# The branch for tokens past an expert's 512th, moved from behind the last expert to ahead of it, with a prefetch hint for TensorE

## The chip, the cores and the metric

One core of one Trainium2 chip runs the kernel. The metric is the device time of one execution in microseconds (us). The engines are TensorE (PE; PEld is its weight load), VectorE (DVE), ScalarE (ACT), GpSimd (POOL) and SyncE (SP, which here only issues DMAs). Each engine has a sequencer that takes its instructions in order: branches, register loads and semaphore waits are done by the sequencer itself, and the profile shows them under the engine's name with a q (PEldq, DVEq, ACTq, POOLq, SPq).

## The reference

```python
def reference(**kwargs):
    ...
    attn_out = _attn_ref(**attn_kwargs)          # windowed causal attention, window 64, 4 x 8 heads x 576 x 64
    x = np.ascontiguousarray(attn_out.transpose(0, 2, 1, 3)).reshape(B * S, H * D)   # 2304 x 512
    x = _moe_ref(x=x, **moe_kwargs)              # relu(x @ w_in) ** 2 @ w_out, d_ff 2048
    return _moe2_ref(x=x, **moe2_kwargs)
def _moe2_ref(x, w_gate, w1, w2):                # 8 experts, each 512 -> 1024 -> 512
    ...
    for e in range(E):
        mask = expert_idx == e                   # expert_idx = argmax of x @ w_gate
        if not mask.any():
            continue
        xe = x[mask]
        h = np.maximum(xe @ w1[e], 0.0)
        ye = h @ w2[e]
        out[mask] = gate_w[mask, None] * ye
    return out.astype(np.float32)
```

## The kernel before

The first two thirds of the program compute the attention and the dense layer and store its result in HBM, and fill a table `tab` that lists the tokens of each expert. What follows, from about 560 us on, is the mixture of experts, and the change lies there.

Every product runs as three matmuls (`mm3`, L167 to L169), because each fp32 number is kept as a rounded part and a rest: rounded by rounded, rounded by rest, rest by rounded. The weights of the next expert are loaded by SP, rounded by ACT (L276), and their rests are made by DVE or POOL (L277), into units of four buffers that two experts in turn use (`wsp[e]`).

`group(e, ...)` computes one expert for up to 512 tokens. It makes eight passes f: `up(f)` (12 matmuls into a PSUM tile h, with the tokens along the free axis), `relu(f)` (ACT writes the rounded part `ggh`, L770, then DVE the rest `ggl`, L771) and `down(f - 1)` (for each of four token tiles t = 3, 2, 1, 0 three matmuls into the PSUM tiles y). TensorE runs `up(f)` ahead of `down(f - 1)`, so ACT and DVE have the time of one `down` or `up` for their part. How wide `up` runs (256, 352, 448 or 512 tokens) and whether a tile of `down` is needed is decided at run time by the expert's token count n, with `tc.If` (L754, L789): the register with n has been loaded on TensorE alone, ahead of the first expert (L1006). Where a tile isn't needed, one tiny matmul with `nil` stands for it.

After `group`, `scatter` is called for the four tiles: DVE multiplies y by the gate weight into an SBUF tile s (L808), and POOL writes its rows to `out` with an indirect DMA (L809).

Experts can have more than 512 tokens. The count of the fullest expert that the groups have to do is in `most`. Behind the last expert stands a condition that every engine evaluates for itself (L1056): it loads `most` into a register and, where it is over 512, runs `more(e, n)` for each expert concerned; that code loads the weights again and works off the rest in tiles of 128 in a loop. With these inputs no count is over 512, so every engine jumps over that code. In the branch that is taken instead, each engine only waits for its own earlier work and raises the semaphores by what the skipped code would have added. POOL does so for the software DMA queues too, and waits for their transfers first; then comes the end of the program (L1097): SP waits for all semaphores, and all engines meet at a barrier behind a DRAIN.

The order of this stage is the order in which the code is written (`tc.manual_schedule()`); the semaphore waits are put in by the framework, which counts what the conditional code may have touched.

Of the kernel before, what the change touches and what calls it, by code (L numbers as in the profile page):

```python
# [19 lines left out]
P = 128  # L20
# [29 lines left out]
def kernel(  # L50
# [13 lines left out]
    nc = tc.nc  # L64
    B, _, NB, W, HP = qT.shape
    D = P // 2
    NT, DM = out.shape
    DFF = w_in.shape[1] // 2
    E, _, F1 = w1.shape
# [6 lines left out]
    KMAX = NT // P  # L76
    GROUP = 4 * P
# [65 lines left out]
    tab = cpool.tile([P, E * KMAX, 2], I32, tag="tab", name="tab")  # L143
    cnt = cpool.tile([1, E], I32, tag="cnt", name="cnt")
    most = cpool.tile([1, 1], I32, tag="most", name="most")
# [4 lines left out]
    def psum(tag, bufs):  # L150
        return pr.tile([P, 512], F32, tag, bufs)

    ybanks = [pspool.tile([P, 512], F32, tag=f"y{i}", name=f"y{i}") for i in range(2 * TT)]
# [7 lines left out]
    def halves(h, l, src):  # L161

        nc.scalar.copy(h, src)
        nc.vector.tensor_tensor(l, src, h.bitcast(F32), op=ALU.subtract)  # L164

    def mm3(o, ah, al, bh, bl, first, last):
        nc.tensor.matmul(o, lhsT=ah, rhs=bh, start=first, stop=False)  # L167
        nc.tensor.matmul(o, lhsT=ah, rhs=bl, start=False, stop=False)  # L168
        nc.tensor.matmul(o, lhsT=al, rhs=bh, start=False, stop=last)  # L169
# [74 lines left out]
    wsp, stg, busiest, done = {}, {}, [], {}  # L244
# [435 lines left out]
    def transposed(x, ps=None):  # L680
        if ps is None:
            ps = psum("a", 2)
        for c in range(4):
            nc.tensor.transpose(ps[:, c * P:(c + 1) * P], x[:, c * P:(c + 1) * P], ident)
        return ps


    def tile_of(e, c0, y, new_r, new_g, between):
        h1, l1, h2, l2 = wsp[e]
        xh, xl = (x[:, :, c0:c0 + P] for x in xhl)  # L690
        hps = [psum("h", 2) for _ in range(2)]

        def up(f, ks):
            for kk in ks:
                b_ = slice(kk * F1 + f * 512, kk * F1 + f * 512 + 512)
                mm3(hps[f], xh[:, kk, :], xl[:, kk, :], h1[:, b_], l1[:, b_], kk == 0, kk == KD - 1)

        def relu(f):
            r = new_r()
            done["relu", f] = nc.scalar.activation(r, hps[f], ACTF.Relu)  # L700
            return r

        def turned(r):
            ps = transposed(r)
            h, l = new_g()
            halves(h, l, ps)
            return h, l

        def down(f, ht, cs):
            for c in cs:  # L710
                a = slice(c * P, c * P + P)
                fc = f * 4 + c
                b_ = slice(fc * DM, fc * DM + DM)
                mm3(y, ht[0][:, a], ht[1][:, a], h2[:, b_], l2[:, b_], fc == 0, fc == 7)

        up(0, range(4))
        r0 = relu(0)
        between(1)
        up(1, range(2))
        t0 = turned(r0)  # L720
        between(3)
        up(1, range(2, 4))
        r1 = relu(1)
        between(4)
        down(0, t0, range(2))
        t1 = turned(r1)
        between(5)
        down(0, t0, range(2, 4))
        down(1, t1, range(4))
# [3 lines left out]
    def group(e, c0, new_g, between, n=None, first=None, after=None):  # L733

        h1, l1, h2, l2 = wsp[e]
        ys = ybanks[2:] if n is None else ybanks
        width = GROUP if n is not None else 2 * P
        hid = {}

        def up(f):  # L740
            hid[f] = psum("h", 2)

            def part(m, ks=range(KD)):
                for kk in ks:
                    b_ = slice(kk * F1 + f * P, kk * F1 + f * P + P)
                    xh, xl = (x[:, kk, c0:c0 + m] for x in xhl)
                    mm3(hid[f][:, :m], h1[:, b_], l1[:, b_], xh, xl, kk == 0, kk == KD - 1)

            def least(sizes):
                if len(sizes) == 1:  # L750
                    part(sizes[0])
                    return
                mid = len(sizes) // 2
                with tc.If(n > sizes[mid - 1]) as c:  # L754
                    least(sizes[mid:])
                with c.Else():
                    least(sizes[:mid])

            if n is not None:
                least(WIDTHS)  # L760
            elif f == 0:
                part(width, range(KD // 2))
                first()
                part(width, range(KD // 2, KD))
            else:
                part(width)

        def relu(f):
            h, l = new_g()
            nc.scalar.activation(h[:, :width], hid[f][:, :width], ACTF.Relu)  # L770
            nc.vector.scalar_tensor_tensor(  # L771
                out=l[:, :width], in0=hid[f][:, :width], scalar=0.0, in1=h[:, :width].bitcast(F32),
                op0=ALU.max, op1=ALU.subtract,
            )
            hid[f] = h, l

        def down(f):
            gh, gl = hid[f]
            b_ = slice(f * DM, f * DM + DM)

            def tile_(t):
                a = slice(t * P, t * P + P)
                mm3(ys[t], gh[:, a], gl[:, a], h2[:, b_], l2[:, b_], f == 0, f == 7)

            for t in reversed(range(width // P)):
                if n is None or t == 0:
                    tile_(t)
                    continue
                with tc.If(n > t * P) as c:  # L789
                    tile_(t)  # L790
                with c.Else():

                    nc.tensor.matmul(ys[t][:, :2], lhsT=nil, rhs=nil[:, :2], start=True, stop=True, skip_group_check=True)

        for f in range(8):
            up(f)
            relu(f)
            if f == 7:
                between(f)
            if f:  # L800
                down(f - 1)
            if f < 7:
                between(f)
        down(7)

    def scatter(y, ent, ys):
        if y is not None:
            nc.vector.tensor_scalar_mul(ys, y, ent[:, 1:2].bitcast(F32))  # L808
        i = nc.gpsimd.indirect_dma_start(  # L809
            out=out[:, :], out_offset=bass.IndirectOffsetOnAxis(ap=ent[:, 0:1], axis=0), in_=ys[:], in_offset=None,  # L810
            bounds_check=NT - 1, oob_is_err=False,
        )
        tc.declare_no_dep(i.ins, group="out", reason="no token is in two tiles")
        tc.add_to_no_dep_group("out", i.ins)
# [77 lines left out]
    for g in range(2 * QB, NS * QB):  # L892
        st, j = divmod(g, QB)
# [7 lines left out]
    last = slot[NS - 1, 0]  # L901
# [11 lines left out]
    for i in range(-PRE, len(order) + LA):  # L913
# [6 lines left out]
        if i >= LA:  # L920
            st, f = order[i - LA]
# [25 lines left out]
    def base(e):  # L947

        return 2 * P * (1 - e % 2)

    def tokens_in(x, c):

        ps = transposed(x).rearrange("p (k t) -> p k t", k=KD)
        halves(*(xx[:, :, c:c + P] for xx in xhl), ps)
# [7 lines left out]
    def new_r():  # L962
        return er.tile([P, HP, P], F32, "s", 3).rearrange("p h s -> p (h s)")

    ns = []
# [57 lines left out]
    def next_of(e):  # L1023
        def between(f):
            if e + 1 == E:
                return
            if f == 5:
                expert_in(e + 1, (0, 1) if base(e + 1) == 0 else (2, 3))
            if f == 7:
                expert_in(e + 1, (2, 3) if base(e + 1) == 0 else (0, 1))  # L1030
            split(e + 1, f, TILES)

        return between

    def more(e, n):

        wsp.pop(e)
        for i in range(8):
            wload(e, i)
            wsplit(e, i, TILES)  # L1040
        with tc.For_i(GROUP // P, (n + (P - 1)) // P, 1) as i:
            ent = rpool.tile([P, 2], I32, tag="ent", name=f"ent{e}")
            nc.vector.tensor_copy(ent, tab[:, ds(e * KMAX + i, 1), :])
            x = new_r()
            nc.vector.memset(x, 0.0)
            gather(x, ent[:, 0:1])
            tokens_in(x, 0)
            tile_of(e, 0, ybanks[0], new_r, new_g, lambda j: None)
            scatter(ybanks[0], ent, new_r())

    with tc.manual_schedule():
        for e in range(E):
            group(e, base(e), new_g, next_of(e), n=ns[e])
            for t in reversed(range(GROUP // P)):
                scatter(ybanks[t], tab[:, e * KMAX + t, :], new_r())
        with tc.If(nc.values_load(most[0:1, 0:1], min_val=0, max_val=NT) > GROUP, preferred_fallthrough_block=False):  # L1056
            for e in range(E):
                n = nc.values_load(cnt[0:1, e:e + 1], min_val=0, max_val=NT)
                with tc.If(n > GROUP):
                    more(e, n)  # L1060


# [38 lines left out]
```

## Time and profile before

| | |
|---|---|
| time, median of 3 runs | 857.18 us (856.23 to 858.75) |
| time of the profiled execution | 855.37 us |
| its span, first to last instruction | 853.7 us |
| TensorE busy | 795.4 us (93% of the span) |
| DVE, ACT, POOL busy | 564.3, 388.0, 274.9 us |
| last matmul of the program | starts at 834.86 us |
| last scatter issued by POOL | starts at 838.06 us |

Times within the profile count from the start of the span. The span lies 1.7 us below the time of the same execution, and the profiled execution itself 1.8 us below the median of the three others. A busy share says how long an engine worked, not whether anything waited for it; what bounds a stretch is read from who waits for whom there.

### The profile page before, as it was taken

What the parts mean: (1) busy time and instruction counts of PE and PEld (TensorE: products, weight loads), DVE (VectorE), ACT (ScalarE), POOL (GpSimd) and SP (SyncE); (2) the same over time, 40 slices, a digit from 0 to 9 for tenths busy, and PEclk for the clock granted to TensorE, in tenths of its full rate; (3) what the DMA queues carried; (4) which work ended last, traced back from release to release, by engine and by line L of the source; (5) the groups of instructions that cost most, each with busy time, mean ns of one, the idle gap of its engine ahead of it and who ended that gap; (6) DMA issues with size and microseconds to landing.
All of it is one profiled execution on the core that took longest, in us unless ns stands there. A gap on an engine that the chain in (4) does not pass through costs nothing. (4 is left out here: it accounts for less than half of the span.)

```text
span 853.7 us, 15131 instructions
## 1 busy us (share of the span) xinstructions
PE 795.4 (93%) x5295; PEld 692.1 (81%) x5295; DVE 564.3 (66%) x1293; ACT 388.0 (45%) x1025; POOL 274.9 (32%) x272
## 2 busy tenths in 40 slices
PE   6878889999999999999999999979998999999991
PEld 5767667988889889898888887868887788888880
DVE  6999995794764947649477396558699763534211
ACT  6986644333443443534444344446566543334110
POOL 4425431112131221312211025366666643431201
PEclk9999999999999999999999999989999999999996
DMA  9854643110211111112111046456476644320101
GB/s 266 279 167 132 190 160 101 43 45 26 68 45 55 45 39 63 50 45 57 35 53 38 13 142 194 137 184 209 144 248 195 218 149 148 120 90 2 46 2 45
DMA packets 50859, 91.49 MB, mean 107 GB/s; under 512 B 8220, under 2 KB 24604, under 8 KB 50752
## 3 DMA queue, kind: packets, MB, share of 16 engines
q1 hardware_dynamic: 44688, 80.43, 30.0%
q0 software_dynamic: 6064, 9.63, 3.4%
q8 instruction: 68, 1.11, 0.5%
q14 instruction: 39, 0.32, 0.1%
HBM read 84.59 MB, written 13.81 MB: 115 GB/s over the span
## 5 line engine op out<-in xcount | busy, mean ns | idle before, releaser
L167 PE MATMUL h<-xh,w 128*128 128x256 f32 (+3 forms) x864 | 262.3, 304 | 16.0 <-DVE gl L479 15.5
L168 PE MATMUL h<-xl,w 128*128 128x256 f32 (+3 forms) x864 | 254.7, 295 | 0.3 <-DVE xl L164 0.3
L169 PE MATMUL h<-xh,w 128*128 128x256 f32 (+3 forms) x864 | 254.8, 295 | 0.0
L167 PEld LDWEIGHTS h<-xh,w 128*128 128x128 f32 x864 | 163.9, 190 | 33.6 <-DVE gl L479 19.7
L168 PEld LDWEIGHTS h<-xl,w 128*128 128x128 f32 x864 | 164.1, 190 | 8.1 <-DVE xl L164 0.8
L169 PEld LDWEIGHTS h<-xh,w 128*128 128x128 f32 x864 | 164.1, 190 | 2.7
L463 ACT ACTIVATE r<-h 128x256 f32<-128x256 f32 x144 | 55.2, 384 | 202.1 <-PE h L169 195.7
L167 PE MATMUL y<-w,gh 128*128 128x512 f32 x294 | 119.3, 406 | 2.2 <-ACT gh L470 2.2
L472 DVE SCALAR_TENSOR_TENSOR h<-h,r 128x256 f32<-128x256 f32 x144 | 61.5, 427 | 84.5 <-ACT r L463 84.4
L168 PE MATMUL y<-w,gh 128*128 128x512 f32 x294 | 116.2, 395 | 0.0
L771 DVE SCALAR_TENSOR_TENSOR ggl<-h,ggh 128x512 fp32r<-128x512 f32 (+1 forms) x69 | 46.0, 667 | 101.2 <-ACT ggh L770 96.7
L770 ACT ACTIVATE ggh<-h 128x512 fp32r<-128x512 f32 (+1 forms) x69 | 40.3, 584 | 148.2 <-PE h L169 114.4
L169 PE MATMUL y<-w,gl 128*128 128x512 f32 x294 | 103.1, 398 | 0.5 <-DVE gl L771 0.5
L549 DVE SCALAR_TENSOR_TENSOR tmp<-tmp,stg 128x512 f32<-128x512 f32 x128 | 95.8, 748 | 0.8
L335 POOL COPY q<-qd 64x256 f32<-64x256 f32 x46 | 32.9, 715 | 150.4 <-PE a L361 149.1
L277 POOL TENSOR_TENSOR w<-stg,w 128x512 fp32r<-128x512 f32 x36 | 48.5, 1354 | 88.1 <-ACT w L276 80.0
L167 PE MATMUL y<-w,ggh 128*128 128x512 f32 x170 | 70.5, 415 | 1.4 <-DVE s L808 0.9
L169 PE MATMUL y<-w,ggl 128*128 128x512 f32 x170 | 67.8, 399 | 2.8 <-DVE ggl L771 2.7
L168 PE MATMUL y<-w,ggh 128*128 128x512 f32 x170 | 66.9, 393 | 0.0
L167 PEld LDWEIGHTS y<-w,gh 128*128 128x128 f32 x294 | 55.9, 190 | 13.2 <-ACT gh L470 3.7
L479 DVE TENSOR_TENSOR gl<-h,gh 128x256 fp32r<-128x256 f32 x144 | 60.6, 421 | 7.6 <-ACT gh L470 1.0
L168 PEld LDWEIGHTS y<-w,gh 128*128 128x128 f32 x294 | 55.8, 190 | 9.6
(157 smaller groups left out, 1306.0 us busy)
## 6 DMA issues: line engine op xcount, KB each, us to landing
stg<-in_moe_w SPq DMA_DIRECT2D x45, 512.0 KB, 4.0
stgx<-in_moe_w SPq DMA_DIRECT2D x18, 512.0 KB, 4.1
stg<-in_moe_w_in SPq DMA_DIRECT2D x16, 512.0 KB, 3.9
stg<-in_moe_w_out SPq DMA_DIRECT2D x16, 512.0 KB, 3.5
v<-in_v SPq DMA_DIRECT2D x28, 256.0 KB, 2.6
x_d<-tmp SPq DMA_DIRECT2D x18, 256.0 KB, 2.0
q<-in_moe_w SPq DMA_DIRECT2D x9, 512.0 KB, 4.1
qd<-in_q SPq DMA_DIRECT2D x28, 128.0 KB, 2.1
```

What stands on the lines that cost most here:

```text
L167: nc.tensor.matmul(o, lhsT=ah, rhs=bh, start=first, stop=False)
L168: nc.tensor.matmul(o, lhsT=ah, rhs=bl, start=False, stop=False)
L169: nc.tensor.matmul(o, lhsT=al, rhs=bh, start=False, stop=last)
L277: rest.tensor_tensor(l[:, a:a + 512], src, h[:, a:a + 512].bitcast(F32), op=ALU.subtract)
L335: nc.gpsimd.tensor_copy(qk[g][rows, :, half, :], d[rows])
L463: nc.scalar.activation(r, gT[st, f][:, :ST], ACTF.Relu)
L472: nc.vector.scalar_tensor_tensor(out=ps[:, ST:2 * ST], in0=ps[:, :ST], scalar=0.0, in1=r, op0=ALU.max, op1=ALU.mult)
L479: nc.vector.tensor_tensor(gl, ps[:, ST:2 * ST], gh.bitcast(F32), op=ALU.subtract)
L549: nc.vector.scalar_tensor_tensor(out=junk, in0=x2sb[tt], scalar=1.0, in1=w, op0=ALU.mult, op1=ALU.mult, accum_out=l[:, t, e:e + 1])
L770: nc.scalar.activation(h[:, :width], hid[f][:, :width], ACTF.Relu)
L771: nc.vector.scalar_tensor_tensor(out=l[:, :width], in0=hid[f][:, :width], scalar=0.0, in1=h[:, :width].bitcast(F32), op0=ALU.max, op1=ALU. ...
```

## The change

The condition with its code becomes a function `rest()` that is called ahead of the last expert (e = 7) instead of behind it. So the same instructions stand between the scatters of expert 6 and the first matmul of expert 7 on each engine. Three things follow in the code. The conditional code may no longer take the weight buffers that expert 7's weights already lie in, so it is given those of expert 6 (`wsp[E - 2]`), and `wsp[E - 1]` is put back behind it. Its tokens go to columns from 512 on of the activation buffers, which expert 7 doesn't use. And the layout of the branch is turned round (`preferred_fallthrough_block=True`): now the skipped code follows the branch directly, and the branch taken lies behind it, next to the code of expert 7. A hint for TensorE's sequencer, which names this branch as likely taken, stands in `down(7)` of expert 6 in both arms of the condition for tile 1.

```diff
@@ -774,6 +774,10 @@
+        def hint(f, t):
+            if e == E - 2 and f == 7 and t == 1:
+                tc.mark_branch_hint_location("rest", hint="LikelyTaken", engines={mybir.EngineType.PE})
+
         def down(f):
...
                 with tc.If(n > t * P) as c:
+                    hint(f, t)
                     tile_(t)
                 with c.Else():
+                    hint(f, t)
...
     def more(e, n):
 
-        wsp.pop(e)
+        wsp[e] = wsp[E - 2]
         for i in range(8):
             wload(e, i)
             wsplit(e, i, TILES)
...
-            tokens_in(x, 0)
-            tile_of(e, 0, ybanks[0], new_r, new_g, lambda j: None)
+            tokens_in(x, 4 * P)
+            tile_of(e, 4 * P, ybanks[0], new_r, new_g, lambda j: None)
             scatter(ybanks[0], ent, new_r())
 
-    with tc.manual_schedule():
-        for e in range(E):
-            group(e, base(e), new_g, next_of(e), n=ns[e])
-            for t in reversed(range(GROUP // P)):
-                scatter(ybanks[t], tab[:, e * KMAX + t, :], new_r())
-        with tc.If(nc.values_load(most[0:1, 0:1], min_val=0, max_val=NT) > GROUP, preferred_fallthrough_block=False):
+    def rest():
+
+        with tc.If(
+            nc.values_load(most[0:1, 0:1], min_val=0, max_val=NT) > GROUP, preferred_fallthrough_block=True, label="rest"
+        ):
+            last = wsp[E - 1]
             for e in range(E):
                 n = nc.values_load(cnt[0:1, e:e + 1], min_val=0, max_val=NT)
                 with tc.If(n > GROUP):
                     more(e, n)
+            wsp[E - 1] = last
+
+    with tc.manual_schedule():
+        for e in range(E):
+            if e == E - 1:
+                rest()
+            group(e, base(e), new_g, next_of(e), n=ns[e])
+            for t in reversed(range(GROUP // P)):
+                scatter(ybanks[t], tab[:, e * KMAX + t, :], new_r())
```

The rows below are the built program's instructions in their order on one engine; `[waits ...]` names the semaphores that an instruction waits for (Activation, DVE, Pool and PE count what those engines have finished, DMASW the software DMAs). A matmul row is a weight load and a matmul.

On TensorE before, from the last tile of expert 6 straight into the two width branches and `up(0)` of expert 7:

```order
L789 UNCONDITIONAL_BRANCH
L167 MATMUL y_130<-w_701,ggh 128x512 [waits Activation_49]
L168 MATMUL y_130<-w_702,ggh 128x512 [waits Pool_49]
L169 MATMUL y_130<-w_701,ggl 128x512 [waits DVE_49]
L754 COMPARE_AND_BRANCH x2
L167 MATMUL h_458<-xh,w_275 128x512 [waits Activation_49]
```

In the change TensorE loads `most` and branches there; the hint stands in front of the six matmuls of tiles 1 and 0:

```order
L793 COMPARE_AND_BRANCH
L1112 BRANCH_PREFETCH_HINT
L167 MATMUL y_131<-w_701,ggh 128x512 [waits Activation_49]
L168 MATMUL y_131<-w_702,ggh 128x512 [waits Pool_49]
L169 MATMUL y_131<-w_701,ggl 128x512 [waits DVE_49]
```

```order
L167 MATMUL y_130<-w_701,ggh 128x512 [waits Activation_49]
L168 MATMUL y_130<-w_702,ggh 128x512 [waits Pool_49]
L169 MATMUL y_130<-w_701,ggl 128x512 [waits DVE_49]
L1060 TENSOR_LOAD most [waits DVE_49]
L1059 COMPARE_AND_BRANCH
```

521 rows further on the branch lands. It waits for TensorE's own matmuls (PE), and the first matmul of expert 7 waits for ACT to have landed too, because the skipped code uses the same PSUM tile:

```order
L1059 UNCONDITIONAL_BRANCH [waits PE_49,PE_sequencer_49]
L754 COMPARE_AND_BRANCH x2
L167 MATMUL h_458<-xh,w_275 128x512 [waits Activation_49]
L168 MATMUL h_458<-xl,w_275 128x512 [waits DVE_49]
L169 MATMUL h_458<-xh,w_276 128x512
```

On ACT in the change, the landing and the first ReLU of expert 7, which now waits for DVE's landing as well as for `up(0)`:

```order
L1059 UNCONDITIONAL_BRANCH [waits Activation_49,Activation_sequencer_49]
L754 UNCONDITIONAL_BRANCH x2
L770 ACTIVATE ggh<-h_458 128x512 [waits DVE_49,PE_49,Activation_49]
L770 ACTIVATE ggh<-h_459 128x512 [waits DVE_49,PE_49,Activation_49]
L793 UNCONDITIONAL_BRANCH x3
```

On POOL before, the end of the program: four scatters, the load and the branch, and an ISA row (it raises the software DMA semaphores) that waits for all transfers:

```order
L809 DMA out<-s_1148,tab 2304x512 [waits DMASW3_49,DVE_49]
L809 DMA out<-s_5402,tab 2304x512 [waits DMASW4_49,DVE_49]
L809 DMA out<-s_1146,tab 2304x512 [waits DMASW5_49,DVE_49]
L809 DMA out<-s_1147,tab 2304x512 [waits DMASW6_49,DVE_49]
L1056 TENSOR_LOAD most [waits DVE_49]
L1056 COMPARE_AND_BRANCH
L1056 ISA [waits Pool_49,Pool_sequencer_49,DMASW4_49,DMASW5_49,DMASW3_49,DMASW6_49,DMASW2_49,DMASW7_49,DMASW1_49,DMASW0_49]
L1056 UNCONDITIONAL_BRANCH
```

In the change nothing but the end of the program follows the last four scatters on POOL; the load, the branch and the ISA row stand behind the scatters of expert 6:

```order
L815 DMA out<-s_1148,tab 2304x512 [waits DMASW3_49,DVE_49]
L815 DMA out<-s_5402,tab 2304x512 [waits DMASW4_49,DVE_49]
L815 DMA out<-s_1146,tab 2304x512 [waits DMASW5_49,DVE_49]
L815 DMA out<-s_1147,tab 2304x512 [waits DMASW6_49,DVE_49]
L1112 UNCONDITIONAL_BRANCH
L1112 ISA [waits barrier_Pool_Activation_PE_DVE_SP_gather]
```

## Rows read from the trace of the kernel before

**Rows 1.** The page, part 1: busy us, share of span, instructions.

```profile
PE 795.4 (93%) x5295; PEld 692.1 (81%) x5295; DVE 564.3 (66%) x1293; ACT 388.0 (45%) x1025; POOL 274.9 (32%) x272
```

**Rows 2.** TensorE's timeline from expert 6 to 7: start us, us, instruction [idle before].

```profile
792.88 0.40 PE L169 MATMUL y<-w,ggl 128*128 128x512 f32 x1
793.11 0.37 PE L167 MATMUL h<-xh,w 128*128 128x448 f32 x1
793.32 0.37 PE L168 MATMUL h<-xl,w 128*128 128x448 f32 x1
```

**Rows 3.** The timelines' last rows of TensorE, DVE and POOL.

```profile
834.86 0.40 PE L169 MATMUL y<-w,ggl 128*128 128x512 f32 x1
...
833.20 2.85 DVE L808 TENSOR_SCALAR s<-y,tab 128x512 f32<-128x512 f32 x4 [2.16 <-PE y L169]
...
838.06 0.97 POOL L809 DMA_INDIRECT out<-s,tab  x1 [0.30 <-issue]
```

**Rows 4.** Sequencers at L1056: count, ns min/median/max, first and last start us.

```profile
L1056 POOLq EVENT_SEMAPHORE  x6: 17/30/43, 836.8 to 841.0; - x6
...
L1056 ACTq COMPARE_BRANCH  x2: 38/44/49, 830.2 to 830.5; - x2
L1056 PEldq COMPARE_BRANCH  x2: 79/1970/3860, 832.6 to 835.6; - x2
L1056 PEldq EVENT_SEMAPHORE  x2: 51/51/51, 835.3 to 835.5; - x2
...
L1056 POOLq COMPARE_BRANCH  x2: 40/40/41, 836.7 to 843.0; - x2
...
L1056 POOLq INC_SWDGE_SEM  x1: 1919/1919/1919, 841.0 to 841.0; - x1
```

**Rows 5.** Sequencers at L1097, the end of the program.

```profile
L1097 SPq EVENT_SEMAPHORE  x14: 17/28/28, 842.9 to 853.6; - x14
L1097 SPq DRAIN  x3: 7/7/13, 843.7 to 853.1; - x3
L1097 POOLq DRAIN  x3: 40/113/7259, 845.5 to 853.4; - x3
L1097 ACTq DRAIN  x2: 8/44/81, 832.9 to 853.1; - x2
L1097 DVEq DRAIN  x2: 10/34/57, 839.9 to 853.1; - x2
```

**Rows 6.** Windows: us, busy (count) by engine, PE clock, DMA share, GB/s.

```profile
845.50:852.80 7.30, 0.00 (x0) 0.00 (x0) 0.00 (x0) 0.00 (x0) 0.00 (x0) 0.50 0.00 1
...
560.80:564.00 3.20, 2.60 (x11) 2.20 (x12) 1.59 (x3) 1.17 (x2) 1.46 (x2) 0.50 0.94 346
564.00:567.40 3.40, 3.40 (x18) 3.27 (x17) 1.54 (x3) 1.17 (x2) 2.56 (x3) 0.50 0.80 283
```

**Rows 7.** Sequencer branches within the experts, and the program's first DRAIN on POOL.

```profile
L789 PEldq COMPARE_BRANCH  x288: 65/176/1210, 570.4 to 831.9; - x144
...
L754 PEldq COMPARE_BRANCH  x160: 65/208/525, 565.1 to 825.7; - x160
...
L1090 POOLq DRAIN  x1: 187/187/187, 0.4 to 0.4; - x1
```

**Rows 8.** ACT, DVE, POOL timelines around the step from expert 6 to 7.

```profile
788.40 1.16 ACT L276 CAST w<-stg 128x512 fp32r<-128x512 f32 x2
795.75 0.60 ACT L770 ACTIVATE ggh<-h 128x512 fp32r<-128x512 f32 x1 [6.19 <-PE h L169]
...
791.27 2.80 DVE L808 TENSOR_SCALAR s<-y,tab 128x512 f32<-128x512 f32 x4 [1.20 <-PE y L169]
...
796.15 0.97 POOL L809 DMA_INDIRECT out<-s,tab  x1 [0.30 <-issue]
```

**Rows 9.** TensorE's timeline ahead of the first expert's tokens.

```profile
557.62 0.40 PE L169 MATMUL y<-w,ggl 128*128 128x512 f32 x1
560.85 0.68 PE L684 MATMUL a<-ident,v 128*128 128x128 f32 x2 [2.83 <-issue]
```

## Prediction

> **What bounds the kernel now.** The page's first part comes first: TensorE is busy for 795.4 us of 853.7 [rows 1], so a pause of TensorE in this stage is paid in full, and work of other engines beside it is free. The change touches two places, and each has its own limit.
>
> At the step from expert 6 to expert 7, TensorE's timeline has no gap: the last matmul of expert 6 runs from 792.88 to 793.28, and the first of expert 7 starts at 793.11, inside its tail [rows 2]. DVE, ACT and POOL have slack there [rows 8].
>
> Behind the last matmul (834.86 + 0.40 = 835.26 us) TensorE no longer matters. DVE multiplies until 833.20 + 2.85 = 836.05, and POOL issues the last scatter from 838.06 to 839.03 [rows 3]. From there to the end of the span, 853.65, nothing is computed: 14.6 us. The sequencer rows say what fills them, all on POOL. Its waits for the transfers end at 841.0; INC_SWDGE_SEM, which raises the semaphores, takes 1.92 to 843.0; the branch follows [rows 4]. The next instruction, a DRAIN, starts at 845.5, so the jump took 2.5. The DRAIN lasts 7.26, to 852.8, and the closing barriers take 0.85 [rows 5]. SP's list of waits ends at 843.7 and the other engines reached their DRAIN by 839.9 [rows 5]: POOL alone holds the end.
>
> **What the change takes away at the end.** Waits, INC_SWDGE_SEM and jump leave POOL's path behind the last scatter. The DRAIN then stands right behind that scatter and can start at 839.03 instead of 845.54: 6.5 us earlier. How long it lasts there is the largest unknown. In its window no engine works and the DMA queues move 1 GB/s [rows 6], so it doesn't wait for data; the only other long look at one is the program's first, 0.19 us, ahead of all DMAs [rows 7]. So its bounds are 0.19 and, if it ends a fixed time after the last scatter, 852.80 - 839.03 = 13.8. I take 7.26: the POOL row nearest to it is itself, and by 845.5 all transfers had been confirmed for 4.5 us, so what it then did was probably its own work. At the short end SP's list sets the end instead. It starts when the last transfer has landed (by 841.0 in rows 4) and takes 843.7 - 842.9 = 0.8 [rows 5]; with the barriers the program would end at 842.7. So this edit gives 6.5, with bounds 0 and 11.0.
>
> POOL's part in its new place is hidden. Its scatters of expert 6 end at 796.15 + 0.97 = 797.1 [rows 8]; landing, INC_SWDGE_SEM and jump took 845.5 - 839.0 = 6.5 behind the last one, so POOL is free by about 804, and its next work is the scatters behind 833.2 [rows 3]. Nothing is queued behind it in between. Without that cover of 29 us it would cost the same 6.5 again. SP has no transfer left to issue; its waits are for loads long landed.
>
> **What it adds between the experts.** TensorE's sequencer now has to load `most`, jump, wait until its own matmuls are done, raise two semaphores and take two width branches before the first matmul of expert 7. Four terms:
>
> 1. The empty queue. At the end of before, the first semaphore step came at 835.3, when the last matmul was done, and the branch behind both at 835.6 [rows 4]: 0.3. Two width branches at a median of 0.21 are 0.4 [rows 7]. So the first matmul starts about 0.7 behind the end of the last one, where it started 0.17 ahead of it [rows 2]. With a start of some 0.1: 1.0 us. Nothing hides it, since nothing may be queued past the wait.
> 2. The jump itself. TensorE's far jump took 3.86 us in before [rows 4], as if the target had to be fetched. The sequencer runs ahead of the array, which covers part: it came to L1056's first branch at 832.6 [rows 4], 2.66 before its last matmul ended. So without a hint 1.2 stay exposed. The hint stands six matmuls further up, ahead of the load; the last branch of that tile was at 831.9 [rows 7], 0.7 earlier. So 0.5 with the hint, between 0 (it is fetched by then) and 1.2 (it is not used).
> 3. The code behind the target. It hasn't been read in order either. If the first stretch ends within `up(0)`, the next one is fetched while twelve matmuls run, at 0.20 each [rows 2] 2.4 us against 3.86 less the 0.7 of term 1: 0.7 exposed. If it reaches further, nothing. In rows 7 the longest branch wait in the experts is 1.21. I take 0.5, with bounds 0 and 1.2.
> 4. ACT and DVE. The first matmul waits for ACT's landing. ACT's last cast ends at 789.56 [rows 8]; its jump took 832.9 - 830.5 = 2.4 [rows 4, 5], so it lands at about 792.2 and is covered by 0.9. DVE landed 839.9 - 836.05 = 3.85 behind its last multiply [rows 3, 5]; from 794.07 [rows 8] that is 797.9. Expert 7's first ReLU waits for it, and stood at 795.75 [rows 8]. With the pause of terms 1 to 3 it is wanted at 797.75, and what it makes is used only one `up` of 2.4 us later. So nothing; if TensorE's pause were under 1 us, this chain would limit it at about 1 us.
>
> Sum of the pause: 1.0 + 0.5 + 0.5 = 2.0, between 1.0 and 3.4. TensorE has nothing idle later in which to win it back, so the end moves by it. The new branch costs the hint and the load beside that, in the sequencer alone.
>
> [...]
>
> **The sum.** 6.5 gained, 2.0 lost: 4.5 faster. Against the profiled execution's own 855.37 that is 850.9; that execution lies 1.8 below the median of 857.18, and the time to be met is a median, so I forecast 852.7. With the bounds of the pause alone, 851.7 to 854.1.
>
> **The rivals.**
>
> *The DRAIN goes too.* If it was long because of INC_SWDGE_SEM or the jump ahead of it, it shrinks at the end. For it: 0.19 at the start of the program. Against it: INC_SWDGE_SEM had ended 2.5 us before. Then 11.0 - 2.0 = 9.0 faster: 848.2.
>
> *The DRAIN is tied to the last scatter (the other side).* If it ends when something of the last indirect DMA has run out, 13.8 us behind that DMA's issue, it lasts longer as it starts earlier. For it: it stands behind 32 scatters and a queue that software runs. Against it: the transfers had landed by 841.0. The price is the whole gain, and only the pause is left: 857.18 + 2.0 = 859.2. It decides from 7.26 + 4.5 = 11.8 us of DRAIN on; between them lies a DRAIN that starts its 7.26 only when the scatters have landed, at 841.0: 4.5 - 2.0 = 2.5 faster, 854.7.
>
> [...]
>
> *The hint does nothing.* Term 2 is 1.2: 853.4. The sign stays.
>
> **How the numbers follow.** The forecast with its variants of the hint has 0.58, the DRAIN gone 0.14, tied to the scatter 0.10, started at the landing 0.08, the fallen clock or a pause beyond 3.4 has 0.10. What a measurement of this kernel can tell from no change is about 0.3%, 2.6 us. The forecast and the DRAIN gone are faster by more, and a part of the landing case: 0.75. The clock, the rest of the landing case, and the tied DRAIN with a pause under 2.6 are the same: 0.18. The tied DRAIN with a longer pause is slower: 0.07. The range goes from 847.8, which takes in the DRAIN gone, to 857.0, which takes in the clock and leaves out the tied DRAIN.
>
> **What would show it.** In the changed profile: POOL's DRAIN at the end starts within 0.3 us of the end of the last scatter and lasts about 7.3; INC_SWDGE_SEM stands near 800; TensorE's timeline has a gap of about 1.5 us ahead of the first matmul of expert 7 and another of under 1 behind `up(0)`; its far branch takes well under 3.86; the last matmul ends at about 837.3; the clock stays at 1.0. The forecast is wrong if the DRAIN has another length, or if TensorE's gaps sum to over 3.4.

## Result and profile after

| | before | changed |
|---|---|---|
| time, median of 6 runs each | 856.7 us (854.73 to 858.75) | 849.38 us (847.54 to 851.94) |
| ratio, 95% interval | | 0.9916 (0.9895 to 0.9938) |
| profiled execution, its span | 855.37, 853.7 us | 849.51, 847.8 us |
| end of the last matmul to the end of the program | 18.4 us | 11.8 us |

The kernel is 7.3 us faster (5.3 to 9.0 by the interval). The forecast was 4.5 faster, to 852.7, between 847.8 and 857.0. So sign and mechanism held, and the gain came out larger.

**The step from expert 6 to expert 7.** TensorE's timeline of the changed kernel, columns as in [rows 2]; the number in brackets is idle time, with what ended it (PEq is TensorE's sequencer):

```profile
792.34 0.39 PE L169 MATMUL y<-w,ggl 128*128 128x512 f32 x1
793.49 0.47 PE L167 MATMUL h<-xh,w 128*128 128x448 f32 x1 [0.76 <-PEq L1059]
793.80 0.36 PE L168 MATMUL h<-xl,w 128*128 128x448 f32 x1
...
795.83 0.36 PE L169 MATMUL h<-xh,w 128*128 128x448 f32 x1
796.09 0.47 PE L167 MATMUL h<-xh,w 128*128 128x448 f32 x1
796.40 0.36 PE L168 MATMUL h<-xl,w 128*128 128x448 f32 x1
```

From start to start, the step takes 793.49 - 792.34 = 1.15 us, where [rows 2] have 793.11 - 792.88 = 0.23: the first pause is 0.92. From the first matmul of expert 7 to the last of the program, before took 41.75 us and this profile 42.08. Most of those 0.33 are lost behind the landing: the two matmuls that follow a stop take 0.31 to the next one in the place of 0.20, and the one at 795.83 takes 0.26. Together the pause is 1.25 us.

What the sequencers did there (L1059 is the branch; columns as in [rows 4]):

```profile
L1059 PEldq EVENT_SEMAPHORE  x2: 51/51/51, 792.8 to 792.9; - x2
L1059 DVEq EVENT_SEMAPHORE  x2: 21/21/21, 796.4 to 796.5; - x2
...
L1059 PEldq COMPARE_BRANCH  x1: 2682/2682/2682, 789.5 to 789.5; - x1
...
L1059 POOLq INC_SWDGE_SEM  x1: 1848/1848/1848, 799.7 to 799.7; - x1
```

TensorE's jump takes 2.68 us where it took 3.86 [rows 4]; it begins at 789.5 and is over at 792.2, half a microsecond ahead of the end of the last matmul (792.34 + 0.39 = 792.73). The semaphore steps stand at 792.8, when the array is empty. DVE lands at 796.4, and ACT's first ReLU starts at 796.54; its result is wanted at 798.66, by `down(0)`. POOL's part is over at 801.5.

**The end.** POOL's timeline and the DRAIN rows of the program's end (now L1112):

```profile
837.49 0.97 POOL L815 DMA_INDIRECT out<-s,tab  x1 [0.30 <-issue]
838.77 0.97 POOL L815 DMA_INDIRECT out<-s,tab  x1 [0.30 <-issue]
```

```profile
L1112 POOLq DRAIN  x3: 40/118/10135, 836.8 to 847.5; - x3
...
L1112 PEldq BRANCH_PREFETCH_HINT  x1: 55/55/55, 788.6 to 788.6; - x1
```

The sequencer comes to the DRAIN while two scatters are still to be issued, so its record is 10.1 us long. So its start says little (the forecast had expected it within 0.3 us of the end of the last scatter), and its end is what counts: 836.80 + 10.14 = 846.93, 7.2 behind the last scatter (838.77 + 0.97 = 839.74). Before, it lasted 7.26 from 845.5 on [rows 5]. The closing barriers follow as before. Two windows of the same profile, expert 7 and the DRAIN (columns as in [rows 6]):

```profile
793.50:835.97 42.47, 42.47 (x192) 35.96 (x192) 7.62 (x12) 4.79 (x8) 3.46 (x4) 1.00 0.07 23
...
839.74:846.97 7.23, 0.00 (x0) 0.00 (x0) 0.00 (x0) 0.00 (x0) 0.00 (x1) 0.50 0.09 36
```

TensorE is busy through all 42.47 us of expert 7 at a granted clock of 1.00, and again no engine works beside the DRAIN.

By the two profiles, then: 18.39 - 11.83 = 6.56 us gained at the end, 1.25 lost at the step, 5.3 in all. The other 0.55 of the difference of the spans (5.86) lies ahead of both: expert 6's last matmul ends at 792.73 here and at 793.28 in [rows 2], and that moment stood anywhere from 790.5 to 795.6 in the thirteen profiles of this study, whatever was changed. But 5.3 is the edge of the interval, and the question was where the rest was.

### The profile page after: what moved, and what is told of

Same layout as the page of the kernel before. It is cut to its first block, busy times and chain, and to the rows that moved or that the text cites. A ratio compares the mean times of both kernels' runs of the same rounds, so it can differ in the third digit from the quotient of the medians.

```text
span 847.8 us, 15128 instructions
## 1 busy us (share of the span) xinstructions
PE 794.2 (94%) x5295; PEld 690.4 (81%) x5295; DVE 563.9 (67%) x1293; ACT 387.9 (46%) x1025; POOL 275.4 (32%) x272
## 4 chain that ended last, share of the span: by engine, by line
PE 65%; issue 13%; DVE 11%; DMA 6%; ACT 2%; POOL 2%; SPq 1%; POOLq 0%; ACTq 0%; DVEq 0%
PE h L167 11%; PE h L168 10%; PE h L169 10%; PE y L167 9%; PE y L169 9%; PE y L168 9%; PE a L361 2%; DMA stg<-in_moe_w_in 2%; PE a L434 2%; DVE tmp L206 2%; DVE tmp L210 1%; DMA vf<-in_v 1%; PE a L684 1%; DVE tmp L202 1%; PE a L419 1%
```

## Experiments

Each ratio is to the kernel before, run beside it on the same chip; its median there was 855.4 us for e1 to e4, 855.5 for e5 to e8 and 854.1 for e9 to e11, so kernels of different groups are compared by their ratios. My account at this point was a DRAIN of fixed length and a pause of 1.25 us; against it stood a DRAIN whose length depends on something, a hint that does nothing, and a gain from elsewhere in the program.

**e1: the hint removed.**

```diff
-                    hint(f, t)
                     tile_(t)
                 with c.Else():
-                    hint(f, t)
```

> The changed kernel without the hint. If the hint is what hid the jump: TensorE's branch takes 3.86 us again (2.68 with the hint), and begins at the same place, 3.2 us ahead of the end of expert 6's last matmul, so it ends 0.6 behind that matmul; the pause ahead of expert 7 grows by 0.5 to 0.7 us, and the program's end with it; the DRAIN stays at 7.2. If TensorE's sequencer has the code at hand anyway, or the hint does nothing: the branch takes 2.7 and the gap stays at 0.76. Either way the whole time stays within 0.3% of the changed kernel's, about 850.

850.17 us, ratio 0.9934 (0.991 to 0.9958). TensorE's branch, and its timeline:

```profile
L1057 PEldq COMPARE_BRANCH  x1: 3778/3778/3778, 790.6 to 790.6; - x1
```

```profile
793.75 0.39 PE L169 MATMUL y<-w,ggl 128*128 128x512 f32 x1
795.21 0.47 PE L167 MATMUL h<-xh,w 128*128 128x448 f32 x1 [1.07 <-PEq L1057]
...
797.55 0.36 PE L169 MATMUL h<-xh,w 128*128 128x448 f32 x1
798.38 0.47 PE L167 MATMUL h<-xh,w 128*128 128x448 f32 x1 [0.47 <-issue]
```

The branch takes 3.78 again and ends at 794.4, 0.2 behind the last matmul. The first pause grows by 0.31, to 1.23, and a second gap stands behind `up(0)`; the whole pause is 2.13. So the hint works. It is worth 0.5 to 0.9 us by these profiles (2.13 against 1.25, and 1.63 in e8), which the times can't show. This is one profile without a hint, and jumps without one differ: at the end of the kernels that keep the condition there, TensorE's took 3.30 (e5), 3.31 (e9), 3.35 (e4), 3.65 (e11) and 3.86 [rows 4], and with the hint of the changed kernel 2.68 to 3.00 in five profiles. Why such a jump takes 3.3 to 3.9 us, no run here shows.

**e2: a DRAIN on POOL where it is idle.**

```diff
                 rest()
+                nc.gpsimd.drain()
             group(e, base(e), new_g, next_of(e), n=ns[e])
```

> The changed kernel with one more DRAIN on POOL, right behind the condition, where POOL has nothing to do for 33 us. If a DRAIN behind software DMAs has a fixed price: the early one takes 7.2 us, hidden, the last one 7.2 too, time as the changed kernel. If its length is work that piles up over the program's software DMAs, or a first-time cost: the early one takes about 7, the last one under 2, and the program ends 5 to 7 us earlier than the changed kernel, near 843. If it waits until a fixed time after the last scatter: the early one, which starts 5 us behind the scatters of expert 6, takes about 2, the last one 7.2.

844.16 us, ratio 0.9863 (0.9838 to 0.9888): faster than the changed kernel by some 5 us. The early DRAIN (L1073), the last one (L1113) and the last scatter:

```profile
L1073 POOLq DRAIN  x1: 6853/6853/6853, 802.8 to 802.8; - x1
```

```profile
L1113 POOLq DRAIN  x3: 46/118/4886, 838.3 to 844.3; - x3
```

```profile
840.28 0.97 POOL L815 DMA_INDIRECT out<-s,tab  x1 [0.30 <-issue]
```

The early one takes 6.85, hidden; the last one ends at 838.3 + 4.89 = 843.2, 1.95 behind the last scatter, where it was 7.2. So the length is neither fixed nor a fixed time behind the last scatter: something had piled up. My forecast had taken the 7.26 as a constant.

**e3: no condition at all** (it leaves out the tokens past an expert's 512th, of which these inputs have none).

```diff
-            if e == E - 1:
-                rest()
             group(e, base(e), new_g, next_of(e), n=ns[e])
```

> The changed kernel without the condition and its code: it leaves out the tokens past an expert's 512th, of which these inputs have none. By my account (tail minus 6.5, pause plus 1.25): the pause goes, TensorE runs from expert 6 into expert 7 without a gap, the tail stays as in the changed kernel (last matmul to end 11.8 us), so 1.2 us faster than the changed kernel, some 848. If the jump or its landing cost something else on the way (weights, ACT, DVE), the gain is larger, 2 us or more. If the pause was not on the path, the time stays.

847.73 us, ratio 0.9905 (0.9885 to 0.9924). TensorE runs on without a gap, as in [rows 2]:

```profile
792.06 0.40 PE L169 MATMUL y<-w,ggl 128*128 128x512 f32 x1
792.29 0.37 PE L167 MATMUL h<-xh,w 128*128 128x448 f32 x1
```

The tail is 11.8 us, as in the changed kernel, and expert 7 takes 41.75 again. So by the profiles 1.25 to 1.6 us of pause are all that the condition costs in its new place; the times, by the ratios 0.9 to 1.9 us less than the changed kernel's, fit that, but the intervals overlap.

**e4: the condition at the end, the layout of its branch turned round.**

```diff
-        with tc.If(... > GROUP, preferred_fallthrough_block=False):
+        with tc.If(... > GROUP, preferred_fallthrough_block=True):
```

> The kernel before with only the layout of the branch turned round: the skipped code follows the branch, the branch taken lies behind it; the condition stays behind the last expert. If the tail is a chain on POOL, its far jump (2.5 us, in before behind the waits for the transfers) now comes first, at the sequencer's run-ahead 836.7, while the last two scatters are still issued: it is hidden, the DRAIN starts at 843.0 instead of 845.5, and the program ends 2.5 us earlier, some 0.3% faster than before. The waits and the raising of the semaphores (1.9 us) stay. If the layout does nothing: as before. If the DRAIN only shifts (it ends when something else has run out), as before too, with a DRAIN of 9.8.

852.67 us, ratio 0.9973 (0.9958 to 0.9988), 2.3 us faster than before. POOL's sequencer:

```profile
L1056 POOLq EVENT_SEMAPHORE  x6: 17/30/43, 838.4 to 840.0; - x6
...
L1056 POOLq COMPARE_BRANCH  x1: 53/53/53, 835.0 to 835.0; - x1
L1056 POOLq INC_SWDGE_SEM  x1: 1928/1928/1928, 840.0 to 840.0; - x1
```

```profile
L1097 POOLq DRAIN  x3: 40/113/7180, 842.0 to 849.8; - x3
```

The jump is now taken at 835.0, beside the scatters, and the DRAIN follows INC_SWDGE_SEM at once. So the 2.5 us of jump were on the path. The waits ended at 840.0, 2.65 us behind the last scatter, where [rows 4] gave 2.0; this was the first sign that this wait has no fixed length.

**e5: the kernel before, with an early DRAIN alone.**

```diff
         for e in range(E):
+            if e == E - 1:
+                nc.gpsimd.drain()
             group(e, base(e), new_g, next_of(e), n=ns[e])
```

> The kernel before, its condition behind the last expert, with one DRAIN on POOL ahead of expert 7 and nothing else. If the DRAIN's length is work piled up by the 87 software DMAs before it (7.26 / 87 = 0.083 us each), independent of the condition: the early one, behind 83 of them, takes 6.9 us, hidden; the last one has four, some 0.3 us, and the end comes 6.9 us earlier than before, near 848.5, with the waits, INC_SWDGE_SEM and jump still on the path. If the short DRAIN of the changed kernel came from the condition's new place: the last one stays at 7.2 here, and the time as before.

847.64 us, ratio 0.9913 (0.9889 to 0.9937): 7.4 us faster, as much as the whole change gains, without it. POOL's rows at the condition and at the end:

```profile
L1058 POOLq EVENT_SEMAPHORE  x6: 17/30/43, 835.2 to 841.3; - x6
...
L1058 POOLq INC_SWDGE_SEM  x1: 259/259/259, 841.4 to 841.4; - x1
```

```profile
L1099 POOLq DRAIN  x3: 46/113/456, 844.5 to 845.5; - x3
```

The early DRAIN (L1054), the last scatter ahead of it and the last scatter of the program:

```profile
L1054 POOLq DRAIN  x1: 9879/9879/9879, 792.6 to 792.6; - x1
```

```profile
794.64 0.97 POOL L809 DMA_INDIRECT out<-s,tab  x1 [0.30 <-issue]
...
836.55 0.98 POOL L809 DMA_INDIRECT out<-s,tab  x1 [0.30 <-issue]
```

The early DRAIN ends at 802.47, 6.86 behind the scatter that ended at 795.61, as forecast. The last DRAIN takes 0.46, with the condition in its old place. INC_SWDGE_SEM shrinks with it, from 1.92 to 0.26, which I hadn't expected. The waits for the transfers ended 3.8 us behind the last scatter here (837.53 to 841.35), and so the tail is 12.0; with the 2.0 us of [rows 4] it would have been 10.2.

**e6: what does a DRAIN count?** The changed kernel with a DRAIN ahead of expert 4 and one behind the condition.

```diff
                 rest()
+                nc.gpsimd.drain()
+            if e == 4:
+                nc.gpsimd.drain()
```

> The changed kernel with two DRAINs more on POOL: ahead of expert 4 (59 of the 87 software DMAs lie behind it by then) and behind the condition (24 more). If each DMA costs the next DRAIN the same: 59 x 0.083 = 4.9 us, then 2.0, and the last one 1.9 behind the last scatter, as with one early DRAIN. If the bytes count (38 and 24 of 62 transfers of a whole tile): 4.2 and 2.6. If it is a first-time cost: 6.8 and under 0.5. The first of them may hold up POOL's share of the weights of expert 5; that is not what is asked here.

One execution, 843.62 us. I had miscounted: of the 87 software DMAs, 63 lie ahead of the first DRAIN, 20 ahead of the second and 4 ahead of the last. The first DRAIN (L1075) and the scatter ahead of it, the second DRAIN, and INC_SWDGE_SEM ahead of the second:

```profile
L1075 POOLq DRAIN  x1: 9368/9368/9368, 669.4 to 669.4; - x1
```

```profile
671.55 1.10 POOL L815 DMA_INDIRECT out<-s,tab  x1 [0.30 <-DVE w L277]
```

```profile
L1073 POOLq DRAIN  x1: 1687/1687/1687, 799.0 to 799.0; - x1
```

```profile
L1059 POOLq INC_SWDGE_SEM  x1: 588/588/588, 798.4 to 798.4; - x1
```

With the right counts, the second should take 20 x 0.083 = 1.7 us if each DMA costs the same, and 20 / 64 of 6.85 = 2.1 if only the transfers of a whole tile do (64 of the 83 behind e2's early DRAIN): it took 1.69. The first (669.39 + 9.37 = 678.76, 6.1 behind the scatter that ended at 672.66, so 6.1 us for 63) is longer than 63 x 0.083 = 5.2. It ran beside loads of weights, at a DMA share up to 0.97, and what its 0.9 more are isn't settled. The last one ends 1.95 behind the last scatter, as in e2.

**e7: the early DRAIN, and the hint one pass sooner.**

```diff
-            if e == E - 2 and f == 7 and t == 1:
+            if e == E - 2 and f == 6 and t == 1:
```

> The changed kernel with the early DRAIN of e2, and the hint one pass earlier (tile 1 of down(6) in the place of down(7) of expert 6, some 5 us sooner). If the 2.7 us of TensorE's branch are the rest of one fetch, it is now at hand: the branch takes 0.1, the sequencer lands 2.6 us sooner, the next stretch of code is fetched sooner too, the branch of 2.1 us in up(0) shrinks and the second gap of 0.2 to 0.3 goes; the first gap, of 0.75, stays, since it is the wait for TensorE's own queue. Whole time as e2, 844, less at most 0.3, which the times can't show. If a hint so early is lost: branch 3.8, both gaps as without a hint.

843.6 us, ratio 0.9866 (0.9838 to 0.9894), as e2. TensorE's sequencer and timeline:

```profile
L1059 PEldq COMPARE_BRANCH  x1: 480/480/480, 787.0 to 787.0; - x1
```

```profile
L1113 PEldq BRANCH_PREFETCH_HINT  x1: 55/55/55, 783.4 to 783.4; - x1
```

```profile
790.07 0.39 PE L169 MATMUL y<-w,ggl 128*128 128x512 f32 x1
791.21 0.47 PE L167 MATMUL h<-xh,w 128*128 128x448 f32 x1 [0.76 <-PEq L1059]
...
793.54 0.36 PE L169 MATMUL h<-xh,w 128*128 128x448 f32 x1
793.74 0.37 PE L167 MATMUL h<-xh,w 128*128 128x448 f32 x1
```

The branch takes 0.48, and the gap behind `up(0)` is gone. The pause is 1.05, of which 0.92 is the step itself, as in the changed kernel: the wait until TensorE's own queue is empty isn't shortened by an earlier landing. From the hint to the end of the branch it took 4.1 us here and 3.6 in the changed kernel (3.8 to 4.0 in e2, e6, e8 and e10), and a jump without a hint takes 3.3 to 3.9. My reading is a fetch of code that the hint starts, while the branch waits for the rest; no row shows it. In the changed kernel's DMA records three packets of program code (8, 16 and 8 KB) moved between 788.75 and 791.46, so between the hint at 788.6 and the end of the branch at 792.2, but they don't say for which engine.

**e8: the changed kernel again.**

> The changed kernel itself, once more, for a second profile and more times. By the account of the two profiles (tail 6.56 shorter, pause 1.25 longer) it is 5.3 us faster than before, a ratio of 0.9938. If something ahead of the last expert gained as well (the first measurement was 7.3 us): 0.991 to 0.992, and the end of expert 6's last matmul stands some 2 us earlier than in other kernels' profiles. If that was chance: it stands anywhere between 791.5 and 794.2, as it did in the profiles so far.

849.25 us, ratio 0.9927 (0.99 to 0.9955), so 6.2 us faster than before. The tail is 11.8 and the DRAIN ends 7.2 behind the last scatter, as in the first profile. The pause is 1.63: the first gap is 0.92 again, the rest lies behind `up(0)`. Expert 6's last matmul ends at 794.79, later than in before. So the profiles show no gain upstream of the change.

**e9: the kernel before again.**

> The kernel before itself, for a second profile. If the profiles give the whole difference: from the end of the last matmul to the end of the program 18.4 us again (11.8 in both profiles of the changed kernel), expert 7 without a pause, and the last matmul of expert 6 ends anywhere between 790 and 795. If the first profile of before had a lucky tail: some 20 us, which would explain that times differ by 6 to 7 us and the profiles' parts sum to about 5.

One execution, 857.3 us. It has a part that the first profile hadn't shown:

```profile
L1056 POOLq EVENT_SEMAPHORE  x6: 17/30/43, 836.7 to 842.9; - x6
...
L1056 POOLq INC_SWDGE_SEM  x1: 1920/1920/1920, 842.9 to 842.9; - x1
```

```profile
L1097 POOLq DRAIN  x3: 40/113/7260, 847.5 to 855.3; - x3
```

```profile
838.04 0.97 POOL L809 DMA_INDIRECT out<-s,tab  x1 [0.30 <-issue]
```

The last scatter ends at 839.01, as in [rows 3], but the waits for the transfers end at 842.9, where they ended at 841.0 [rows 4]. So the tail is 20.35 us, 2.0 longer, with the same INC_SWDGE_SEM, jump and DRAIN, and the span is 1.9 longer. How often the wait is that long isn't known: this execution took longer than all seven others of this kernel on that chip (853.0 to 855.1).

**e10: 20 software DMAs more, of 8 bytes each,** behind the condition.

```diff
                 rest()
+                for i in range(20):
+                    nc.gpsimd.dma_start(tab_d[i:i + 1, :], tab[0:1, i, :])
```

> The changed kernel with 20 software DMAs more, of 8 bytes each, on POOL behind the condition, where POOL is idle. If each software DMA costs the next DRAIN the same, whatever it carries: the last DRAIN ends 107 x 0.083 = 8.9 us behind the last scatter (7.2 without them). If bytes or rows count: 7.2 to 7.3.

```profile
L1114 POOLq DRAIN  x3: 40/118/11883, 838.3 to 850.8; - x3
```

```profile
840.42 0.98 POOL L815 DMA_INDIRECT out<-s,tab  x1 [0.30 <-issue]
```

One execution, 852.82 us. The DRAIN ends at 838.34 + 11.88 = 850.22, 8.8 us behind the last scatter (841.40). So 20 DMAs of 8 bytes added 1.6 us, 0.08 each: it counts DMAs, not bytes.

**e11: e4 and e5 together,** the condition at the end.

> The kernel before with an early DRAIN ahead of expert 7 and the branch's layout turned round, the condition left behind the last expert: e4 and e5 together, without the move. If the parts add up: from the last matmul to the end 16.4 (e4) less 6.7 (DRAIN 7.2 to 0.45) less 1.7 (INC_SWDGE_SEM 1.93 to 0.26) = 8.0 us, no pause ahead of expert 7, so some 10.4 us faster than before, 845, the same as the move with an early DRAIN (7.1 us of tail and 1.0 to 1.4 of pause). If the move is needed for the gain: 850 or more.

843.24 us, ratio 0.9861 (0.9845 to 0.9878).

```profile
L1058 POOLq INC_SWDGE_SEM  x1: 268/268/268, 844.2 to 844.2; - x1
```

```profile
L1099 POOLq DRAIN  x3: 46/113/381, 844.5 to 845.8; - x3
L1099 SPq DRAIN  x3: 7/7/13, 845.1 to 845.5; - x3
```

The tail is 8.5 us, 0.5 more than forecast: 0.2 of it is the wait, which took 2.8, and 0.3 is SP. POOL's DRAIN is over at 844.86, but SP's list of waits only at 845.1, so POOL no longer holds the end alone. There is no pause. So the move isn't needed: the early DRAIN and the layout give as much as the move with an early DRAIN (e2, e7).

All kernels side by side, in us: the time of the runs (of one execution for e6, e9 and e10), the rest from one trace each. The pause is what step and expert 7 take beyond 0.23 and 41.75 us; the wait is from the end of the last scatter to INC_SWDGE_SEM, where that stands at the end. The DRAIN is counted from its start in the first five rows, and from the end of the last scatter, which the sequencer doesn't wait for, in the others; n is the number of software DMAs issued since the DRAIN before it.

| | time | pause | wait | INC_SWDGE_SEM | last DRAIN (n) | last matmul to end |
|---|---|---|---|---|---|---|
| before | 856.7 | 0 | 2.0 | 1.92 | 7.26 (87) | 18.4 |
| e9, before again | 857.3 | 0 | 3.9 | 1.92 | 7.26 (87) | 20.4 |
| e4, layout | 852.67 | 0 | 2.65 | 1.93 | 7.18 (87) | 16.4 |
| e5, DRAIN | 847.64 | 0 | 3.8 | 0.26 | 0.46 (4) | 12.0 |
| e11, both | 843.24 | 0 | 2.8 | 0.27 | 0.38 (4) | 8.5 |
| changed | 849.38 | 1.25 | | | 7.2 (87) | 11.8 |
| e8, changed again | 849.25 | 1.63 | | | 7.2 (87) | 11.8 |
| e1, no hint | 850.17 | 2.13 | | | 7.2 (87) | 11.8 |
| e3, no condition | 847.73 | 0 | | | 7.2 (87) | 11.8 |
| e10, 20 DMAs more | 852.82 | 1.35 | | | 8.8 (107) | 13.6 |
| e2, early DRAIN | 844.16 | 1.38 | | | 1.95 (4) | 7.1 |
| e6, two DRAINs | 843.62 | 1.1 | | | 1.95 (4) | 7.1 |
| e7, and early hint | 843.6 | 1.05 | | | 1.95 (4) | 7.1 |

## Why the prediction was right, and what it mis-sized

**The tail, forecast 6.5.** The step was right: the DRAIN stands behind the last scatter, with its full 7.2 us. In the first two profiles it gained 6.56. That the DRAIN kept its length was partly luck: the forecast took the 7.26 as a constant, for want of a nearer row, while e2, e5, e6 and e10 show that the count of software DMAs sets it, and the move leaves that at 87. But the sum took the wait for the transfers from one row, 2.0 us. In the five profiles in which POOL waits for them at the end it took 2.0, 3.9, 2.65, 3.8 and 2.8, on average 3.05, so [rows 4] had the shortest; in the kernel before itself it was 2.0 and 3.9. In the changed kernel SP's list still waits for the transfers, but beside the DRAIN (the list ended at 842.1, the DRAIN at 846.9), so it costs nothing there. With 3.05, the gain is 3.05 + 1.92 + 2.5 = 7.5.

The DMA records of the traces show that this wait isn't only chance. In the eight profiles without the condition at the end, the last transfer landed 1.74 to 1.76 us behind the end of the last scatter, in every one. In the five with it there, it landed 1.8, 3.7, 2.45, 3.6 and 2.6 behind, and only those five move packets of program code (8 and 16 KB) while the last scatter is issued and lands. In e9 and e5 the late rows of the scatter start within 0.02 us of the end of such a packet, one of 16 KB that took 1.6 us in each. So the code that is loaded for the condition probably delays the scatters there; no run tests that.

**The pause, forecast 2.0.** Term 1 (the empty queue, 1.0, with 0.1 for a start that no row gave) measured 0.92 in every kernel with a hint but e6, where it was 0.97. Term 2 (the jump, 0.5) was 0: the sequencer came to the branch 3.2 us ahead of the end of the array's work, not 2.66, and the jump took 2.68 with the hint. The 3.86 that stood for a jump without one was the longest of six (3.30 to 3.86). Term 3 (the code behind the target, 0.5) was 0.33 and 0.71 in the two profiles of the changed kernel; a width branch (L754) took up to 2.01 and 2.39 us there, against 0.53 in before [rows 7], but that this is a fetch was an estimate that no row shows. Term 4 (ACT and DVE, 0) held: the ReLU started late, at 796.54, and `down(0)` didn't wait for it. So 1.25 to 1.63, inside the bounds of 1.0 to 3.4.

**The sum.** 7.5 less 1.25 to 1.63 is 5.9 to 6.3 us. The times gave 7.3 (5.3 to 9.0) and 6.2 (3.9 to 8.6). That the gap between the forecast 4.5 and the measurement comes from these two terms is therefore consistent; the times can't tell 6 from 7.

**The rivals.** The DRAIN didn't vanish by itself, and it isn't tied to the last scatter (7.2 behind it here, 13.8 in before). Nor does it start its 7.2 when the scatters have landed: the last transfer landed at 841.49 by the DMA records, so it would have ended at 841.49 + 7.26 = 848.75, and it ended at 846.9. TensorE's clock didn't fall: the window of expert 7 above shows a granted clock of 1.00. The upper end of the range, 857.0, took in a fallen clock; no run shows that term, and step and expert 7 together took at most 2.13 us more than in before (e1). The hint does something (e1, e7). I called the 7.26 us POOL's own work; the runs show a price per software DMA, which neither forecast nor rivals had.

## What to carry to other kernels

Read the end of a program in the sequencers' rows, engine by engine: here 14.6 us lay behind the last issue, all of them on POOL. The condition there cost less where its engines had other work (the tail 6.56 us shorter, the pause 1.25 to 1.63 longer), but two smaller edits together did more: turning the branch's layout so that its jump is taken early (2.3 us), and a DRAIN on POOL while it is idle, which takes off what the last DRAIN would do (5 to 7 us, alone as much as the move). The best kernels, e2, e7 and e11, are 11 to 12 us faster than before. And a wait for transfers at the end is not a constant: it took 2.0 us in one profile of the kernel before and 3.9 in the other, so one profile isn't enough to size it.

## What the runs showed of the hardware

- POOL's DRAIN behind software DMAs took 0.38 to 0.46 us for 4 of them, 1.69 for 20, 6.85 for 83 and 7.26 for 87: about 0.08 us each, also for those of 8 bytes (e10).
- INC_SWDGE_SEM grows with the same count: 0.26 (4), 0.59 (20), 1.85 (83), 1.92 (87), some 0.02 us each on top of some 0.2, and a DRAIN resets it too.
- A DRAIN that the sequencer reaches while scatters are still being issued ended 1.95 us behind the last of them (e2, e6 and e7), though only 4 DMAs were left. That is 0.2 us behind the landing of the last transfer in all three traces (843.00, 840.35 and 839.01), so it fits a DRAIN that waits for the landing as well; as the landing stood at 1.74 each time, a fixed delay behind the scatter isn't ruled out.
- From a prefetch hint on TensorE to the end of its branch it took 3.6 to 4.1 us in six profiles, whether the hint stood about 1 or 3.6 us ahead of the branch. The branch itself took 2.68 to 3.00 us in five of them and 0.48 in e7, with the earlier hint: what was left of that time.
